# A pair's first four transposes, in the same step as its keys' sums (attention and a mixture of experts, one core)

## The chip, the cores and the metric

The kernel runs on one core of a Trainium2 chip. The time is device microseconds of one execution. The core's engines work side by side: TensorE (matmuls and transposes through the matrix array), ScalarE, VectorE, GpSimd, and SyncE, which here issues transfers. Each engine takes its instructions in the order in which the program emits them and waits by semaphores for the others.

## What is computed

Attention with random features for 4 batches of 8 heads (576 positions, 64 channels, 128 features), then four experts' two-layer networks on its output:

```python
def phi(x):
    proj = np.einsum('bhsd,md->bhsm', x, omega)
    sq = np.sum(x * x, axis=-1, keepdims=True) / 2.0
    h = proj - sq
    h = h - np.max(h, axis=-1, keepdims=True)
    return np.exp(h) / np.sqrt(m)
q_p, k_p = (phi(q_s), phi(k_s))
kv = np.einsum('bhsm,bhsd->bhmd', k_p, v)
z = np.sum(k_p, axis=2)
num = np.einsum('bhsm,bhmd->bhsd', q_p, kv)
den = np.einsum('bhsm,bhm->bhs', q_p, z)[..., None] + 1e-06
...
for e in range(E):
    h = np.maximum(x @ w1[e], 0.0)
    out += p[:, e:e + 1] * (h @ w2[e])
```

All is float32.

## The kernel before

Two heads make a pair, so each batch has four pairs. Batch 0 is done in an opening of its own (`begin`). The twelve pairs of batches 1 to 3 are cut into small steps by the generator `later_ticks`; each `yield` ends a step. The driver in `emit` runs the experts' work in pieces (a "visit" is one expert's half of its hidden units on a block of rows) and calls `next(ticks)` behind a piece as often as a fixed ratio says: 76 steps over 45.4 units of expert work for batches 1 and 2 (`over` is true), 54 steps over the first block of the larger visits for batch 3 (`over` is false). The order in which instructions are emitted is the order on each engine; nothing reorders it afterwards.

The steps of one pair, as far as they matter here:

- `project("q")` (L411): TensorE multiplies the queries with the features into two PSUM banks, one for each head. VectorE takes the maxima (L279, L284) and makes the bias (L289, L290).
- `exp_tails("q")`, `exp("q", 0)` (L417, L418): ScalarE makes the exponentials, two for the tails and four for the first head (L296). Then, a step later, `exp("q", 1)` (L424): four for the second head.
- `sum_keys()` (L430): TensorE accumulates the keys' sums (L310, L314; the trace has two records for each float32 matmul, 2 + 16), ScalarE copies them (L316), VectorE takes what the copy lost (L317). In the same step the next pair's values are loaded and its keys squared on GpSimd.
- `turn(0)` (L437): TensorE transposes four tiles of the queries' exponentials (L325): the first two of the first head, then the first two of the second head, into one PSUM bank. ScalarE copies it (L335) and VectorE takes the difference (L336). With `over`, the next pair's queries are squared on GpSimd in the same step.
- `turn(1)` (L441): the other four and the tail (L325, L329).

The results of `turn(0)` are used by `numerators(0)`, in the next pair's first step with `over`, and two steps behind `turn(0)` without.

The experts' matmuls are L674 to L676 and L867 (first layer), L689 to L691 and L942 (second layer); each weight tile is split into a high and a low part by ScalarE (L498) and GpSimd (L501). All PSUM tiles come from one pool of eight banks in turn.

Of the kernel before, what the change touches and what calls it, by code (L numbers as in the profile page):

```python
# [14 lines left out]
def attention_moe(ctx, tc, kT, qT, kd, qd, kn, qn, vn, omT, probs, w1, w2, out):  # L15
# [372 lines left out]
    def later_ticks(pairs, over):  # L388

        before = None  # L390
        for p, then in zip(pairs, pairs[1:] + [None]):
            p.project("k")
            p.project_tails("k")
            p.maxima("k")
            p.maxima_tails("k")
            p.bias("k")
            if before:
                before.numerators(0)
            yield
            p.exp_tails("k")  # L400
            p.exp("k", 0)
            p.lengths("q")
            if before:
                before.invert(0)
            yield
            p.exp("k", 1)
            if before:
                before.times(0)
                before.numerators(1)
            yield  # L410
            p.project("q")  # L411
            p.project_tails("q")
            p.maxima("q")
            p.maxima_tails("q")
            p.bias("q")
            yield
            p.exp_tails("q")  # L417
            p.exp("q", 0)  # L418
            if before:
                before.invert(1)  # L420
            if then:
                then.load("k")
            yield
            p.exp("q", 1)  # L424
            if before:
                before.times(1)
            if then:
                then.load("q")
            yield
            p.sum_keys()  # L430
            if then:
                then.load_v()
                if then.hp == 0:
                    then.load_tails()
                then.square("k")
            yield
            p.turn(0)  # L437
            if over and then:
                then.square("q")
            yield  # L440
            p.turn(1)  # L441
            if then:
                if over:
                    then.lengths("k")
                else:
                    then.square("q")
            yield
            if over and then:
                before = p
                continue  # L450
            before = None
            p.numerators(0)
            if then:
                then.lengths("k")
            yield
            p.invert(0)
            p.times(0)
            p.numerators(1)
            yield
            p.invert(1)  # L460
            p.times(1)
            yield
# [849 lines left out]
    def emit():  # L1312
        pairs, g1 = begin()
        later = [Halves(b, hp) for b in range(1, B) for hp in range(NP)]
        windows = {
            0: (first_rest(pairs, opening(later[0])), 15 / 11),
            3: (later_ticks(later[:-NP], True), 76 / 45.4),
            N0: (chain(opening(later[-NP]), later_ticks(later[-NP:], False)), 54 / (NV * (BIG[1][1] // P + 1) * 0.8)),
        }
        ticks, n, done, per = iter(()), 0, 0.0, 0  # L1320
        for v in range(len(visits)):
            if v in windows:
                for _ in ticks:
                    pass
                ticks, per = windows[v]
                n, done = 0, 0.0
            for share in first_visit(g1) if v == 0 else fast(v) if v >= N0 else plain(v):
                done += share
                while n < done * per:
                    next(ticks, None)  # L1330
                    n += 1
        store(0)
# [61 lines left out]
```

## Time and profile before

| | us |
|---|---|
| Median of 3 runs | 891.69 |
| Lowest and highest run | 889.99, 892.38 |
| The profiled execution | 892.62 |
| Its span, first to last instruction | 890.8 |
| TensorE busy | 884.1 |
| VectorE, GpSimd, ScalarE busy | 593.8, 566.3, 468.9 |

The span is 1.8 us shorter than the execution that it belongs to. Starts are in microseconds from the span's first instruction. A matmul's record is longer than the time that it holds TensorE, because matmuls overlap: how fast they go is read from one start to the next. A record that follows a wait or a block of short matmuls starts early, while its weights are loaded.

### The profile page before, as it was taken

Reading aid. Unit: us, or ns where it says so; the run is one execution under the profiler, and the core shown is the slowest. Engines: PE = TensorE matmul, PEld = TensorE weight load, DVE = VectorE, ACT = ScalarE, POOL = GpSimd, SP = SyncE. Lnnn points to the kernel's source line nnn. Section 1 sums busy time; section 2 is a strip of 40 time slices with the busy share of each in tenths; the row PEclk is TensorE's granted clock in tenths of the full one; section 3 lists DMA queues with packets and bytes.
Section 4 is the critical chain, followed back from the end, with each engine's and each line's share of the span. In section 5 each row is a group of like instructions: output and inputs, shape, how many; then the busy total and the mean of one; then the engine's idle time right before and its main releaser. Section 6 shows DMA issues by size and latency. Waiting matters only on the chain.

```text
span 890.8 us, 14823 instructions
## 1 busy us (share of the span) xinstructions
PE 884.1 (99%) x5484; PEld 789.4 (89%) x5484; DVE 593.8 (67%) x1026; ACT 468.9 (53%) x1038; POOL 566.3 (64%) x494
## 2 busy tenths in 40 slices
PE   9999999999999999999999999999999999999998
PEld 9988888888888898989889899898989898998988
DVE  5765566766767646586766666975848476675847
ACT  5564676776774564546545554634443435444442
POOL 6656465555634554444445346779898888979874
PEclk9999999999999999999999999999999999999999
DMA  6664454444521757436275353835152442425132
GB/s 179 165 204 153 127 170 135 150 154 137 160 80 60 254 154 274 181 135 246 77 273 175 111 211 111 305 117 165 48 178 87 139 157 80 155 60 178 44 135 95
DMA packets 64552, 134.01 MB, mean 150 GB/s; under 512 B 10624, under 2 KB 21056, under 8 KB 64480
## 3 DMA queue, kind: packets, MB, share of 16 engines
q1 hardware_dynamic: 54512, 102.95, 35.3%
q0 software_dynamic: 9360, 29.82, 10.3%
q8 instruction: 43, 0.70, 0.3%
q10 hardware_dynamic: 608, 0.30, 0.1%
q14 instruction: 29, 0.24, 0.1%
HBM read 98.96 MB, written 34.08 MB: 149 GB/s over the span
## 4 chain that ended last, share of the span: by engine, by line
PE 90%; DVE 4%; issue 2%; DMA 2%; ACT 1%; POOL 1%; SPq 0%; POOLq 0%; ACTq 0%; DVEq 0%
PE g L867 26%; PE g L942 17%; PE g L689 8%; PE g L691 7%; PE g L690 7%; PE g L674 3%; PE g L676 3%; PE g L675 3%; PE kv L314 2%; PE q_ps L266 1%; PE k_ps L266 1%; DMA kept<-w1ah 1%; PE qt_ps L325 1%; PE k_ps L147 1%; PE q_ps L147 1%
## 5 line engine op out<-in xcount | busy, mean ns | idle before, releaser
L501 POOL TENSOR_TENSOR w2l<-w2r,w2h 128x512 fp32r<-128x512 f32 x93 | 123.9, 1337 | 81.6 <-ACT w2h L498 69.8
L718 DVE SCALAR_TENSOR_TENSOR acc<-g,pr,acc 128x256 f32<-128x256 f32 (+1 forms) x278 | 139.2, 539 | 31.7 <-PE g L691 21.8
L501 POOL TENSOR_TENSOR w1sl<-w1r,w1sh 128x512 fp32r<-128x512 f32 (+1 forms) x43 | 75.2, 1749 | 72.3 <-ACT w1sh L498 56.8
L689 PE MATMUL g<-w2h,hh 128*128 128x512 f32 x280 | 112.7, 402 | 0.4 <-ACT kp L296 0.2
L691 PE MATMUL g<-w2h,hl 128*128 128x512 f32 x280 | 109.8, 392 | 0.0
L690 PE MATMUL g<-w2l,hh 128*128 128x512 f32 x280 | 109.5, 391 | 0.0
L879 DVE TENSOR_TENSOR sum<-g,sum 128x384 f32<-128x384 f32 (+1 forms) x96 | 59.3, 619 | 63.1 <-PE g L867 56.4
L892 DVE SCALAR_TENSOR_TENSOR hl<-sum,hh 128x384 fp32r<-128x384 f32 (+1 forms) x64 | 45.7, 717 | 81.7 <-ACT hh L888 52.3
L867 PE MATMUL g<-xbh,w1sh 128*128 128x384 f32 (+1 forms) x256 | 93.1, 364 | 0.0
L867 PE MATMUL g<-xbl,w1sh 128*128 128x384 f32 (+1 forms) x256 | 92.9, 363 | 0.0
L867 PE MATMUL g<-xbh,w1sl 128*128 128x384 f32 (+1 forms) x256 | 92.6, 362 | 0.0
L501 POOL TENSOR_TENSOR w1al<-w1r,w1ah 128x512 fp32r<-128x512 f32 (+1 forms) x45 | 51.5, 1159 | 52.1 <-ACT w1ah L498 36.7
L873 ACT ACTIVATE sum<-g 128x384 f32<-128x384 f32 (+1 forms) x96 | 50.7, 541 | 51.9 <-PE g L867 51.0
L867 PE MATMUL g<-xbh,w1ah 128*128 128x384 f32 (+1 forms) x192 | 70.1, 365 | 0.0
L498 ACT ACTIVATE w2h<-w2r 128x512 fp32r<-128x512 f32 x90 | 55.2, 627 | 28.2 <-DMA w2r<-in_w 22.1
L867 PE MATMUL g<-xbl,w1ah 128*128 128x384 f32 (+1 forms) x192 | 69.6, 362 | 0.0
L867 PE MATMUL g<-xbh,w1al 128*128 128x384 f32 (+1 forms) x192 | 69.5, 362 | 0.0
L691 PEld LDWEIGHTS g<-w2h,hl 128*128 128x128 f32 x280 | 52.5, 188 | 11.9 <-DVE hl L925 0.4
L689 PEld LDWEIGHTS g<-w2h,hh 128*128 128x128 f32 x280 | 52.7, 188 | 11.2 <-DVE sum L879 0.7
L690 PEld LDWEIGHTS g<-w2l,hh 128*128 128x128 f32 x280 | 52.7, 188 | 8.7
L888 ACT ACTIVATE hh<-sum 128x384 fp32r<-128x384 f32 (+1 forms) x64 | 35.0, 550 | 41.6 <-DVE sum L879 41.2
L867 PEld LDWEIGHTS g<-xbh,w1sh 128*128 128x128 f32 x256 | 48.1, 188 | 6.0 <-DVE sum L879 0.6
(212 smaller groups left out, 2438.5 us busy)
## 6 DMA issues: line engine op xcount, KB each, us to landing
w2r<-in_w SPq DMA_DIRECT2D x108, 256.0 KB, 2.9
w1r<-in_w SPq DMA_DIRECT2D x38, 512.0 KB, 3.6
kept<-w1sh SPq DMA_DIRECT2D x16, 512.0 KB, 4.9
kept<-w1sl SPq DMA_DIRECT2D x16, 512.0 KB, 5.5
w1sh<-kept POOLq DMA_DIRECT2D x16, 512.0 KB, 5.8
w1sl<-kept POOLq DMA_DIRECT2D x16, 512.0 KB, 6.6
kept<-w1ah SPq DMA_DIRECT2D x16, 384.0 KB, 4.3
kept<-w1al SPq DMA_DIRECT2D x16, 384.0 KB, 4.5
```

Of the source, the lines that this page charges most:

```text
L498: hi.activation(a, t, AF.Copy)
L501: lo.tensor_tensor(c, t, f32(a), ALU.subtract)
L689: nc.tensor.matmul(ps, ha[:, ts_], wa, start=(c == 0), stop=False)
L690: nc.tensor.matmul(ps, ha[:, ts_], wc, start=False, stop=False)
L691: nc.tensor.matmul(ps, hc[:, ts_], wa, start=False, stop=(c == FH - 1))
L718: nc.vector.scalar_tensor_tensor(to, ps, sc, to, ALU.mult, ALU.add)
L867: nc.tensor.matmul(ps, a[:, w], x[:, k], start=(start and k + at == 0), stop=(k == 1 and at == 2), skip_group_check=not start)
L873: nc.scalar.activation(t, P_[g][where], AF.Copy)
L879: nc.vector.tensor_tensor(t, P_[g][where], t, ALU.add)
L888: nc.scalar.activation(ha, t, AF.Relu)
L892: nc.vector.scalar_tensor_tensor(x, y, 0.0, f32(z), ALU.max, ALU.subtract)
L942: nc.tensor.matmul(to, x, w, start=(start and f + k == 0), stop=(f + k == 3), skip_group_check=not start)
```

## The change

The end of a step is moved behind `turn(0)`, so that the step of `sum_keys()` holds the four transposes and what follows them on ScalarE and VectorE too. The step behind it keeps the squaring of the next pair's queries where `over` is true (batches 1 and 2) and is empty in batch 3. The number of steps is as before.

```diff
                 if then.hp == 0:
                     then.load_tails()
                 then.square("k")
-            yield
             p.turn(0)
+            yield
             if over and then:
                 then.square("q")
             yield
```

## Rows read from the trace of the kernel before

**Rows 1.** The page: busy time of each engine, and the last chain by engine

```profile
PE 884.1 (99%) x5484; PEld 789.4 (89%) x5484; DVE 593.8 (67%) x1026; ACT 468.9 (53%) x1038; POOL 566.3 (64%) x494
...
PE 90%; DVE 4%; issue 2%; DMA 2%; ACT 1%; POOL 1%; SPq 0%; POOLq 0%; ACTq 0%; DVEq 0%
```

**Rows 2.** TensorE's waits: releaser, then us in total, times, longest us

```profile
PE g L942 <- DVE hl L925: 0.7, 2, 0.5
```

**Rows 3.** Timeline of TensorE, pair 1: start us, us, line, tiles, shape, count

```profile
99.83 0.39 PE L690 MATMUL g<-w2l,hh 128*128 128x512 f32 x1
100.05 0.39 PE L691 MATMUL g<-w2h,hl 128*128 128x512 f32 x1
100.28 0.60 PE L325 MATMUL qt_ps<-ident,qp 128*128 128x128 f32 x4
100.64 0.47 PE L689 MATMUL g<-w2h,hh 128*128 128x512 f32 x1
100.95 0.40 PE L690 MATMUL g<-w2l,hh 128*128 128x512 f32 x1
```

**Rows 4.** Timeline of TensorE in the opening, transposes right behind a pair's sums

```profile
19.51 0.61 PE L190 MATMUL qt_ps<-ident,qp 128*128 128x128 f32 x4
19.95 0.28 PE L147 MATMUL q_ps<-om,q 128*128 128x128 f32 x1
```

**Rows 5.** Timelines of ScalarE, weight loads and TensorE: TensorE waiting for exponentials

```profile
41.99 0.37 ACT L162 ACTIVATE qp<-q_ps,nm 128x128 f32<-128x128 f32 x1 [1.25 <-DVE nm L150]
...
42.41 1.17 PEld L190 LDWEIGHTS qt_ps<-ident,qp 128*128 128x128 f32 x5 [0.18 <-ACT qp L162]
...
385.70 0.50 PE L689 MATMUL g<-w2h,hh 128*128 128x512 f32 x1 [0.18 <-ACT kp L296]
386.04 0.39 PE L690 MATMUL g<-w2l,hh 128*128 128x512 f32 x1
```

**Rows 6.** Timelines of ScalarE and TensorE, pair 3

```profile
143.53 0.65 ACT L296 ACTIVATE qp<-q_ps,nbq 128x128 f32<-128x128 f32 x2
...
143.88 0.39 PE L675 MATMUL g<-x_first,w1sh 128*128 128x512 f32 x1
```

**Rows 7.** Timelines of VectorE, ScalarE and TensorE, pair 7

```profile
230.77 1.02 DVE L289 SCALAR_TENSOR_TENSOR mxq<-sqq,mxq 128x9 f32<-128x9 f32 x1
...
233.87 1.66 ACT L296 ACTIVATE qp<-q_ps,nbq 128x128 f32<-128x128 f32 x6
...
234.69 0.39 PE L675 MATMUL g<-x_first,w1sh 128*128 128x512 f32 x1
```

**Rows 8.** Timelines of GpSimd, VectorE, ScalarE and TensorE, pair 10

```profile
388.94 2.39 POOL L501 TENSOR_TENSOR w1sl<-w1r,w1sh 128x1024 fp32r<-128x1024 f32 x1 [5.33 <-ACT w1sh L498]
...
389.85 1.50 DVE L289 SCALAR_TENSOR_TENSOR mxq<-sqq,mxq 128x9 f32<-128x9 f32 x1
...
391.66 0.74 ACT L303 ACTIVATE qp<-t_ps,nbq 64x128 f32<-64x128 f32 x2 [2.79 <-DVE nbq L290]
...
393.73 0.39 PE L690 MATMUL g<-w2l,hh 128*128 128x512 f32 x1
...
395.11 0.61 ACT L296 ACTIVATE qp<-q_ps,nbq 128x128 f32<-128x128 f32 x2
```

**Rows 9.** Timelines of VectorE, ScalarE and TensorE, pair 12

```profile
497.43 1.88 DVE L289 SCALAR_TENSOR_TENSOR mxq<-sqq,mxq 128x9 f32<-128x9 f32 x1
...
500.36 1.66 ACT L296 ACTIVATE qp<-q_ps,nbq 128x128 f32<-128x128 f32 x6
...
501.05 0.39 PE L690 MATMUL g<-w2l,hh 128*128 128x512 f32 x1
```

**Rows 10.** Timelines of ScalarE and TensorE, pair 9

```profile
344.99 1.66 ACT L296 ACTIVATE qp<-q_ps,nbq 128x128 f32<-128x128 f32 x6
...
347.36 0.39 PE L690 MATMUL g<-w2l,hh 128*128 128x512 f32 x1
```

**Rows 11.** Bias line of the queries: duration ns min/median/max, first and last start

```profile
L289 DVE SCALAR_TENSOR_TENSOR mxq<-sqq,mxq x12: 169/170/1880, 94.1 to 497.4; 128x9 f32<-128x9 f32 x12
```

More of the change, by code (lines that the diff above doesn't have):

```diff
@@ L435, in later_ticks @@
                 then.square("k")
+            p.turn(0)
             yield
-            p.turn(0)
             if over and then:
```

## The prediction, made before the changed kernel was built or run

> **What bounds the kernel now.** I read the shares of the page first, then the list of TensorE's waits, then the order of TensorE around the edited lines. TensorE is busy for 884.1 of 890.8 us, and the chain that ended last is 90% TensorE [rows 1]. Nothing hides a TensorE stall: behind the opening the largest entry in the list of its waits is 0.7 us in two waits [rows 2]. So a microsecond in which TensorE stands still costs very nearly a microsecond, and the question is whether the new order makes it stand still.
>
> The reader should see next how TensorE runs there. In the first of the twelve pairs the sums of the keys are followed by six 512-column matmuls of the experts, then by the four transposes [rows 3], which show the last two of the six. The experts' matmuls start 0.22 to 0.24 us apart; I use 0.23. The change takes the matmuls that stand between sums and transposes and puts them behind the transposes; the rows show one pair, and in the trace all twelve have 6 to 24 such matmuls there, so the edit bites in every pair.
>
> **Part 1, TensorE's own work.** Nothing is added or removed. In the old place the four transposes cost, from 100.28 to the second matmul behind them at 100.95 less one step of 0.23, 100.72 - 100.28 = 0.44 us [rows 3]. In the new place they stand right behind fp32 matmuls of the sums. The opening has just that neighbourhood: sums end, transposes start at 19.51, the next matmul at 19.95, so 0.44 us again [rows 4]. Difference 0.00 per pair. The bounds come from the matmul behind a block of short ones, whose successor is 0.31 instead of 0.23 us away [rows 3]: if one such exit of 0.08 us went in each pair the gain would be 12 x 0.08 = 1.0 us, and if one were added it would be as large a loss. I take 0, since the transposes' 0.44 us already is that excess.
>
> **Part 2, the new wait.** The first two transposes read exponentials of the first head, the last two the first two of the four that ScalarE makes for the second head. Today the experts' matmuls stand between and cover that. In the new order they don't. I compare two times in each pair. F is when TensorE is through with the sums: the start of the second matmul behind them, less 0.23 (the first one's record begins early, while its weights load). E is when the second of the last four exponentials ends.
>
> Without a wait, F + 0.44 is where the next expert matmul streams. With one, TensorE goes on late: in the opening an exponential that starts at 41.99 and takes 0.37 is followed by the load of its transpose at 42.41, 0.05 after its end [rows 5]. Then the last transpose's load (0.11, the step in rows 4) is exposed, and so is the next matmul's: after a wait the first matmul is 0.34 from the second where 0.23 is normal, 0.11 more [rows 5]. So the next matmul streams at E + 0.05 + 0.22, and the loss is E - F - 0.17 where that is positive.
>
> - Pair 3: F = 143.88 - 0.23 = 143.65, E = 143.53 + 0.65 = 144.18. Loss 0.36 us [rows 6].
> - Pair 7: F = 234.69 - 0.23 = 234.46, E = 233.87 + 1.66 = 235.53. Loss 0.90 us [rows 7].
> - Pair 10: F = 393.73 - 0.23 = 393.50, E = 395.11 + 0.61 = 395.72. Loss 2.05 us [rows 8].
> - Pair 12: F = 501.05 - 0.23 = 500.82, E = 500.36 + 1.66 = 502.02. Loss 1.03 us [rows 9].
> - The other eight come out negative. The nearest is pair 9: E = 344.99 + 1.66 = 346.65 against F = 347.36 - 0.23 = 347.13, 0.65 us to spare [rows 10].
>
> Sum 4.3 us. What is queued behind the waiting transposes on TensorE is the whole expert stream, since it issues matmuls in order; later waits that could swallow part of it are the 0.7 us above, and those end on engines that TensorE itself feeds, so I let them absorb nothing.
>
> **Why E is late, and whether that will repeat.** In pair 10 VectorE's small bias instruction takes 1.50 us where the median of its line is 0.17 [rows 11]. It starts at 389.85 and ends at 391.35, and GpSimd's split of a weight tile runs from 388.94 to 391.33 [rows 8]. In pair 12 it is 1.88 us [rows 9], in pair 7 1.02 us [rows 7]. The exponentials wait for the bias: in pair 10 ScalarE stood idle for 2.79 us until it came [rows 8]. So the delays are inside E: 1.50 - 0.17 = 1.33 in pair 10, 1.71 in pair 12, 0.85 in pair 7.
>
> The Trainium skill, page "SBUF — State Buffer", section "SBUF: two separate sides", says that VectorE with two SBUF inputs and GpSimd contend for one pair of ports, which the first to start holds for its whole instruction while the other is blocked. The rows of pair 10 agree: the bias instruction ends 0.02 us after GpSimd's. By that rule the delay is the remainder of GpSimd's instruction and the sum is 4.3 us; if the two shared the ports, the delays would nearly go and the sum would be the 1.1 us of the rival below.
>
> The collisions sit before the edited step, between parts that the edit does not move: in pair 10 VectorE's additions feed ScalarE's split, that feeds GpSimd's, and the bias comes later in the same VectorE order. I therefore expect them to recur.
>
> **Part 3, the other queues.** ScalarE's copy of the transposes and VectorE's difference of it move ahead of the experts' next activations and accumulations, and the PSUM bank is taken one turn earlier. What stands behind is the ReLU of a hidden block (six steps of 0.23, so 1.4 us after the transposes, longer than the copy) or an accumulation, whose bank comes round eight turns later. So the cover is there; if it failed, the bound from the nearest rows is one bias-like collision of the same two engines, 1.3 us once, and below zero there is nothing to win, as TensorE waits for neither today [rows 2]. I take 0. No DMA moves; the loads, GpSimd's squares and SyncE's queue keep their places. In the last batch one step is left empty, which issues nothing.
>
> **Sum.** The profiled execution took 892.62 us, 1.8 more than its span of 890.8. 892.62 + 4.3 = 896.9. It is 0.93 us above the median of the runs (891.69), so for a median I say 896.0 us, 0.48% slower.
>
> **Rivals.**
> - *The collisions don't recur* (not slower). The place is the bias instruction in pairs 7, 10 and 12. Without them E is earlier by 0.85, 1.33 and 1.71: pair 7 loses 0.05, pair 12 nothing, pair 10 0.72, pair 3 still 0.36. Sum 1.1 us, median 892.8. It decides as soon as 1.6 us of the 4.3 goes, which takes two of the three collisions (0.85, 1.33 and 1.03 us of loss). Against it: the order that makes them is untouched; for it: they hang on starts that lie 0.9 us apart in pair 10 [rows 8]. Chance 0.13.
> - *The transposes wait for all of the last four exponentials.* Two more at a step of about 0.26 each, so 0.5 us in each of four pairs: 4.3 + 2.1 = 6.4, median 898.1. Pair 9 would still have 0.14 to spare. Against it, in the opening the first transpose's load starts 0.05 us after the first exponential, and the five loads follow at a step of (1.17 - 0.14) / 4 = 0.26, not all at once behind the last [rows 5]. Chance 0.11.
> - *The order matters to nothing*: the transposes' wait is covered because the last exponentials come earlier once ScalarE has one copy less in its way, or an exit is saved (part 1). 890.7 to 891.7. Against it: in pair 10 ScalarE had stood idle until the bias came [rows 8], so it is not a backlog of copies that makes E late. Chance 0.08.
>
> That the edit does nothing is excluded by the 6 to 24 matmuls counted above.
>
> **How the numbers follow.** Forecast 0.68, around 896.0 with about 1.3 either way (one pair's wait more or less). 0.3% is about what a measurement of this kernel can tell from no change: 2.7 us, so "slower" starts at 894.4. Slower: the forecast without its lower edge, 0.66, and the second rival, 0.11: 0.77. Same: 0.13 of the first rival, 0.05 of the third, 0.02 of the forecast's edge: 0.20. Faster: 0.03. The range goes from just below the first rival's 892.8 to just above the second's 898.1: 892.3 to 899.0.
>
> **What would show it.** In the changed kernel's TensorE waits a new line must stand, transposes waiting for the exponentials, with four entries (pairs 3, 7, 10 and 12), the longest near 2 us in pair 10, and eight pairs without any. The four transposes behind the sums should still take 0.44 us in those eight. The prediction is wrong if no such entry stands there, if the pairs that wait are others, or if the bias instruction has 0.17 us in pairs 7, 10 and 12.

## The result: slower by half a per cent

| | us |
|---|---|
| Changed kernel, median of 10 runs | 894.7 (892.94 to 896.27) |
| Kernel before, median of 10 runs on the same chip | 889.8 (888.57 to 892.57) |
| Ratio | 1.0052, 95% interval 1.0041 to 1.0063 |
| Profiled execution of the changed kernel, its span | 894.11, 892.3 |

The changed kernel is slower by 0.52%, 4.6 us of 889.8; the medians themselves lie 4.9 us apart. The spans of the two profiled executions differ by 1.5 us only, and that is not the change: the one of before had a slow opening (last section). So the comparison that follows runs from the first pair's sums to the last pair's last transpose. The view of one line's instructions has both ends; of the changed kernel (first two rows) and of the kernel before (last two; duration in ns, then first and last start in us):

```profile
L310 PE MATMUL kv<-vb,kp x24: 377/378/378, 94.7 to 500.1; 128*128 128x256 f32 x24
L329 PE MATMUL qt_ps<-ident,qp x12: 272/273/273, 100.5 to 509.5; 128*128 128x128 f32 x12
...
L310 PE MATMUL kv<-vb,kp x24: 377/378/378, 96.7 to 498.8; 128*128 128x256 f32 x24
L329 PE MATMUL qt_ps<-ident,qp x12: 272/273/273, 102.5 to 507.2; 128*128 128x128 f32 x12
```

That is 509.5 - 94.7 = 414.8 us, and in the kernel before 507.2 - 96.7 = 410.5 us. The stretch of the twelve pairs is 4.3 us longer.

The page and the list of TensorE's waits, after:

```profile
PE 883.4 (99%) x5484; PEld 788.1 (88%) x5484; DVE 593.6 (67%) x1026; ACT 467.6 (52%) x1038; POOL 564.5 (63%) x494
...
PE 83%; DVE 6%; ACT 4%; issue 3%; POOL 3%; DMA 1%; SPq 0%; POOLq 0%; ACTq 0%
...
PE qt_ps L325 <- ACT qp L296: 2.7, 4, 1.4
...
PE g L942 <- DVE hl L925: 0.7, 2, 0.5
```

TensorE does the same number of matmuls in the same busy time, to 0.7 us [rows 1]; the chain that ended last now passes through ScalarE, VectorE and GpSimd for 13% of the span where it was 6%. Behind the opening the list has one new line: transposes (L325) that wait for the exponentials (L296), four times. The entry of [rows 2] is unchanged.

Where they are is seen in TensorE's timeline: pair 1, which does not wait, and then pairs 3, 7, 10 and 12.

```profile
96.89 0.60 PE L325 MATMUL qt_ps<-ident,qp 128*128 128x128 f32 x4
97.24 0.48 PE L689 MATMUL g<-w2h,hh 128*128 128x512 f32 x1
97.56 0.40 PE L690 MATMUL g<-w2l,hh 128*128 128x512 f32 x1
...
141.68 0.38 PE L325 MATMUL qt_ps<-ident,qp 128*128 128x128 f32 x2
142.52 0.59 PE L325 MATMUL qt_ps<-ident,qp 128*128 128x128 f32 x2 [0.46 <-ACT qp L296]
...
143.18 0.40 PE L675 MATMUL g<-x_first,w1sh 128*128 128x512 f32 x1
...
233.32 0.39 PE L325 MATMUL qt_ps<-ident,qp 128*128 128x128 f32 x2
234.15 0.58 PE L325 MATMUL qt_ps<-ident,qp 128*128 128x128 f32 x2 [0.44 <-ACT qp L296]
...
234.81 0.40 PE L675 MATMUL g<-x_first,w1sh 128*128 128x512 f32 x1
...
393.18 0.38 PE L325 MATMUL qt_ps<-ident,qp 128*128 128x128 f32 x2
394.93 0.59 PE L325 MATMUL qt_ps<-ident,qp 128*128 128x128 f32 x2 [1.37 <-ACT qp L296]
...
395.59 0.39 PE L690 MATMUL g<-w2l,hh 128*128 128x512 f32 x1
...
502.14 0.55 PE L325 MATMUL qt_ps<-ident,qp 128*128 128x128 f32 x2
503.14 0.58 PE L325 MATMUL qt_ps<-ident,qp 128*128 128x128 f32 x2 [0.45 <-ACT qp L296]
...
503.79 0.39 PE L690 MATMUL g<-w2l,hh 128*128 128x512 f32 x1
```

In pair 1 the four transposes stand in one row and take 97.56 - 0.23 - 96.89 = 0.44 us, as in [rows 3] and [rows 4]. In the four others the row is split: two transposes of the first head, a gap, two of the second head. The gap that the profile prints in brackets is shorter than the loss, because a matmul's record goes on after the next one could have started (a transpose's record is 0.27 us, and in pair 1 the next one starts after 0.11). The loss is read as in the prediction, from the start of the second expert matmul less 0.23, less the first transpose's start, less 0.44: 143.18 - 0.23 - 141.68 - 0.44 = 0.83 in pair 3, and likewise 0.82 in pair 7, 1.74 in pair 10, 0.98 in pair 12. Together 4.4 us, which is the 4.3 of the whole stretch.

### The profile page after: what moved, and what is told of

Its sections match the earlier page's. It is cut to its first block, busy times and chain, and to the rows that moved or that the text cites. A ratio compares the mean times of both kernels' runs of the same rounds, so it can differ in the third digit from the quotient of the medians.

```text
span 892.3 us, 14822 instructions
## 1 busy us (share of the span) xinstructions
PE 883.4 (99%) x5484; PEld 788.1 (88%) x5484; DVE 593.6 (67%) x1026; ACT 467.6 (52%) x1038; POOL 564.5 (63%) x494
## 4 chain that ended last, share of the span: by engine, by line
PE 83%; DVE 6%; ACT 4%; issue 3%; POOL 3%; DMA 1%; SPq 0%; POOLq 0%; ACTq 0%
PE g L867 29%; PE g L942 17%; PE g L689 7%; PE g L691 7%; PE g L690 7%; PE g L674 2%; PE g L675 2%; PE g L676 2%; PE kv L314 1%; PE k_ps L266 1%; PE qt_ps L325 1%; PE kv L177 1%; PE q_ps L266 1%; PE nd L207 1%; POOL w2l L501 1%
```

## The experiments

The theory is that the cost is the wait of the transposes for the second head's exponentials, in four pairs. The rivals: that the order costs something in every pair (the copies of ScalarE and VectorE ahead of the experts' work, another neighbour for the transposes), and, behind the theory, that the exponentials are late for another reason than the collisions of VectorE and GpSimd. All ratios are to the kernel before, run beside them.

| Kernel | Ratio (95%) | Pairs' stretch, us | Transposes' waits in TensorE's list |
|---|---|---|---|
| before | 1 | 410.5 | none |
| the change | 1.0052 (1.0041 to 1.0063) | 414.8 | 2.7 us, 4 |
| pairs 3, 7, 10, 12 alone | 1.0060 (1.0044 to 1.0077) | 414.6 | 2.9 us, 4 |
| the other eight alone | 1.0001 (0.9989 to 1.0012) | 410.5 | none |
| transposes alone moved | 1.0056 (1.0040 to 1.0072) | 414.3 | 2.5 us, 4 |
| change, maxima in PSUM | 1.0011 (0.9998 to 1.0023) | 411.8 | 0.7 us, 2 |
| change, exponentials together | 1.0031 (1.0020 to 1.0042) | 412.4 | 0.9 us, 2 |
| change, both | 0.9997 (0.9988 to 1.0006) | 409.9 | none |
| before, both | 0.9990 (0.9979 to 1.0001) | 410.1 | none |

**In which pairs.** The change was cut in two, once for the pairs named and once for the rest:

```diff
-            p.turn(0)
+            early = (4 * p.b + p.hp - 3) in (3, 7, 10, 12)
+            if early:
+                p.turn(0)
             yield
+            if not early:
+                p.turn(0)
             if over and then:
                 then.square("q")
```

(`not in` for the other eight.)

> The change in pairs 3, 7, 10 and 12 alone; the other eight keep the order of before. If the cost is TensorE's wait for the last exponentials, all of it is here: those four waits stand in the trace of the changed kernel with 0.8, 0.8, 1.7 and 0.9 us, so 4.2 us and some 0.5% over the kernel before. If the new order costs something in every pair (copies of ScalarE and VectorE moved ahead, another neighbour for the transposes), a third of 4.6 us: 1.5 us, 0.2%.

> The change in the other eight pairs (1, 2, 4, 5, 6, 8, 9, 11) alone. If the cost is the wait, these have none and the time is that of before, within 1 us, with no wait of transposes for exponentials in TensorE's list. If each pair costs the same, two thirds of 4.6 us: 3.1 us, 0.35%.

The first costs what the change costs, 1.0060, and has the same wait (first row below); the second costs nothing, 1.0001, and the largest entry behind the opening in its list is the second row, the one of [rows 2]:

```profile
PE qt_ps L325 <- ACT qp L296: 2.9, 4, 1.6
```

```profile
PE g L946 <- DVE hl L929: 0.7, 3, 0.3
```

(The edit moves later lines by four.) Eight pairs with the new order, copies and all, are free; four carry the whole cost. An order that costs in every pair is out.

**The copies.** Here TensorE's transposes move as in the change, while the copies stay in the step where they were:

```diff
             p.turn(0)
             yield
+            p.turn_copies(0)
```

where `turn_copies` is the part of `turn` behind the transposes.

> TensorE's four transposes are moved as in the change, in all pairs; ScalarE's copy and VectorE's difference of them stay in the step where they were. If the wait is the cause, the time is that of the change, 4 to 5 us over before, with the same four waits in TensorE's list. If the copies that moved ahead on ScalarE and VectorE are the cause, the time is near that of before.

1.0056, and the wait stands (2.5 us, four times). The copies that moved ahead on ScalarE and VectorE have no visible part in it.

**Why the exponentials are late.** The maxima go into unused columns of the tails' PSUM bank, so that the two bias instructions (L289, L290) read only one operand from SBUF:

```diff
-            for x in ("mx", "nb"):
-                setattr(self, x + which, att.tile([P, 9], F32, tag=x + which, name=x + which))
+            setattr(self, "nb" + which, att.tile([P, 9], F32, tag="nb" + which, name="nb" + which))
+            setattr(self, "mx" + which, self.t_ps[0][:, 2 * M:2 * M + 9])
```

> The change, and the maxima of a projection in unused columns of its tails' PSUM bank in place of SBUF, so that the two bias instructions read one SBUF operand and one of PSUM. If they are late because they read two SBUF operands beside a split of GpSimd, the bias takes about 0.2 us in every pair, the waits in pairs 3, 7 and 12 go and pair 10 keeps 1.7 - 1.1 = 0.6 us: 0.6 us over before. If they are late for another reason, the four waits and the 4 to 5 us stay.

1.0011, with the four waits down to two. The bias line of this kernel, its VectorE and GpSimd in pair 10, its waits, and its TensorE in pairs 3 and 10:

```profile
L289 DVE SCALAR_TENSOR_TENSOR t_ps<-sqq,t_ps x12: 172/172/173, 93.4 to 498.0; 128x9 f32<-128x9 f32 x12
...
389.65 0.17 DVE L289 SCALAR_TENSOR_TENSOR t_ps<-sqq,t_ps 128x9 f32<-128x9 f32 x1
389.86 0.17 DVE L290 SCALAR_TENSOR_TENSOR nbq<-sqq,t_ps 128x9 f32<-128x9 f32 x1
...
388.10 2.41 POOL L501 TENSOR_TENSOR w1sl<-w1r,w1sh 128x1024 fp32r<-128x1024 f32 x1 [4.45 <-ACT w1sh L498]
...
PE qt_ps L325 <- ACT qp L296: 0.7, 2, 0.4
...
PE k_ps L266 <- DMA k<-in_kd: 0.6, 1, 0.6
...
142.65 0.38 PE L325 MATMUL qt_ps<-ident,qp 128*128 128x128 f32 x2
...
143.93 0.40 PE L675 MATMUL g<-x_first,w1sh 128*128 128x512 f32 x1
...
393.04 0.38 PE L325 MATMUL qt_ps<-ident,qp 128*128 128x128 f32 x2
...
394.51 0.39 PE L690 MATMUL g<-w2l,hh 128*128 128x512 f32 x1
```

GpSimd's split runs from 388.10 to 390.51. The bias instruction starts in the middle of it, as in [rows 8], and takes 0.17 us instead of 1.50: across all twelve pairs 172 or 173 ns, where [rows 11] had a maximum of 1880. The edit moves this instruction's output to PSUM too, but that is not the reason: the one behind it (L290) still writes to SBUF, runs beside the same split and takes 0.17 us as well. So two SBUF operands beside a GpSimd instruction were the cause of the long bias, and that part of the forecast, read there from rows, is now shown.

Pairs 7 and 12 don't wait any more. Pair 10 loses 394.51 - 0.23 - 393.04 - 0.44 = 0.80 us, where 0.6 was expected, and pair 3 143.93 - 0.23 - 142.65 - 0.44 = 0.61 us, where none was: the maxima in PSUM have a price, in the last section, which may be the reason. The wait for a transfer of keys (L266) is one that no other of these profiles has. With the two losses it comes to 2.0 us, while the stretch is only 1.3 us longer than before; the 0.4 us by which the stretch of "before, both" is shorter, with its maxima in PSUM too, is a part of the rest.

**ScalarE's order.** The last four exponentials are emitted right behind the first head's:

```diff
             p.exp("q", 0)
+            p.exp("q", 1)
             if before:
                 before.invert(1)
             ...
             yield
-            p.exp("q", 1)
             if before:
                 before.times(1)
```

> The change, and the last four exponentials of the queries one step earlier, right behind the four of the first head, so that no split of weights stands between them on ScalarE. If TensorE waits for the second of these four, pair 10 goes from 1.7 to about 0.1 us and pair 3 to none, while pairs 7 and 12, where they already follow each other, keep 0.8 and 0.9: 1.9 us over before in place of 4 to 5. If ScalarE's order is not what TensorE waits for, 4 to 5 us stay.

1.0031, and two waits are left, in pairs 7 and 12 (losses of 0.81 and 0.98 us). ScalarE in pair 10 of the change between the two heads' exponentials (first row), and ScalarE and TensorE of this kernel:

```profile
393.56 1.06 ACT L498 ACTIVATE w1sh<-w1r 128x1024 fp32r<-128x1024 f32 x1 [0.59 <-issue]
...
391.15 2.17 ACT L296 ACTIVATE qp<-q_ps,nbq 128x128 f32<-128x128 f32 x8
393.16 1.11 ACT L498 ACTIVATE w1sh<-w1r 128x1024 fp32r<-128x1024 f32 x1
...
392.52 0.67 PE L325 MATMUL qt_ps<-ident,qp 128*128 128x128 f32 x4
...
393.27 0.39 PE L690 MATMUL g<-w2l,hh 128*128 128x512 f32 x1
```

The split of a weight tile, 1.1 us of ScalarE behind 0.59 us in which it stood idle, was between the two heads' exponentials. Now it stands behind them, and the four transposes are one row: pair 10 loses 393.27 - 0.23 - 392.52 - 0.44 = 0.08 us, although its bias still takes 1.23 us. So in pair 10 the late bias and ScalarE's order carried the wait together: with the bias on time 0.80 us were left, with the other order almost nothing.

**Both, with the change and without it.**

> The change, with the maxima in PSUM and the last exponentials one step earlier. If both parts of the delay are understood, no transposes wait for exponentials and the time is that of before within 1 us; if the new order has a cost of its own, it is what is left.

> The kernel before with the same two edits (maxima in PSUM, last exponentials one step earlier) and without the change: what these edits cost or bring by themselves. Expected: nothing, within 1 us of before, since no transposes wait there. If exponentials that come earlier hold up a ReLU on ScalarE that TensorE waits for, it is slower by that, up to 1 us in a pair.

With both edits the changed order costs nothing: 0.9997, no transposes wait for exponentials, and its stretch is 409.9 us against 410.1 without the change. The cost of the change is its waits and nothing else that these runs can see (their intervals are about 1 us either way). The two edits by themselves bring at most 0.2%, and their interval reaches past 1: a faster kernel is not shown.

## Why the prediction was right

- **Part 1** (no change in TensorE's own work) holds: 0.44 us for the four transposes in the new place, and eight pairs that cost nothing.
- **Part 2** named the four pairs, and they are the four. Its sum was 4.3 us; measured are 4.4 in the rows of the waits, 4.3 over the stretch and 4.6 (3.6 to 5.6) by the ratio of the runs. Term by term it was less good: 0.36, 0.90, 2.05 and 1.03 forecast, 0.83, 0.82, 1.74 and 0.98 found. Two misses of about half a microsecond and of a third cancelled, and that is luck: the same four waits come to 4.6 us in the trace of "pairs 3, 7, 10, 12 alone" and to 4.1 in that of "transposes alone moved". The rule for the loss, E - F - 0.17, is good to 0.05 us: with E from the changed kernel's own trace (142.73, 234.36, 395.13 and 503.34) and F the start of the first transposes it gives 0.88, 0.87, 1.78 and 1.03. What was off is E.
- *Pair 3* was mis-sized because E was taken from one execution of the kernel before as fixed. In it a collision lies one stage earlier, at the bias of the keys, which the forecast had not looked at. GpSimd and VectorE there, before (two rows) and after (two rows):

```profile
128.60 2.54 POOL L501 TENSOR_TENSOR w2l<-w2r,w2h 128x512 fp32r<-128x512 f32 x2
130.60 0.56 DVE L289 SCALAR_TENSOR_TENSOR mxk<-sqk,mxk 128x9 f32<-128x9 f32 x1
```

```profile
127.16 2.54 POOL L501 TENSOR_TENSOR w2l<-w2r,w2h 128x512 fp32r<-128x512 f32 x2
128.61 1.12 DVE L289 SCALAR_TENSOR_TENSOR mxk<-sqk,mxk 128x9 f32<-128x9 f32 x1
```

  GpSimd's two splits end at 131.14 and 129.70, and the bias with them. VectorE came to it 2.00 us after GpSimd's start before and 1.45 after, so it waited 0.56 us longer. The exponentials of the keys, the ReLU behind them and the queries' bias follow later by the same half microsecond: the ReLU starts 141.44 - 137.23 = 4.21 us ahead of the pair's sums before, 139.47 - 135.78 = 3.69 after.

  The change is not needed for such a shift. Up to that bias the kernel with "pairs 3, 7, 10, 12 alone" emits in the order of before, and "the other eight alone" in the order of the change; the same instruction in their profiles:

```profile
130.69 1.08 DVE L289 SCALAR_TENSOR_TENSOR mxk<-sqk,mxk 128x9 f32<-128x9 f32 x1
```

```profile
130.32 0.34 DVE L289 SCALAR_TENSOR_TENSOR mxk<-sqk,mxk 128x9 f32<-128x9 f32 x1
```

  So one order gave 0.56 and 1.08 us, the other 1.12 and 0.34. With "transposes alone moved" it was 0.86, and pair 3 lost 0.57 us where it lost 0.83 in the change. The loss of pair 3 differs from one execution to the next by a quarter of a microsecond or more, and rows of one profile can't forecast it closer. What shifts GpSimd against VectorE stays open.
- *Pair 10* was over by 0.3: GpSimd's split began 1.19 us ahead of the bias instead of 0.91 [rows 8], so the collision was 1.23 us, not 1.50:

```profile
388.36 2.39 POOL L501 TENSOR_TENSOR w1sl<-w1r,w1sh 128x1024 fp32r<-128x1024 f32 x1 [5.06 <-ACT w1sh L498]
...
389.55 1.23 DVE L289 SCALAR_TENSOR_TENSOR mxq<-sqq,mxq 128x9 f32<-128x9 f32 x1
```

  Here the order of the other pairs seems to count. Where the eight pairs keep the old order the collision is 1.50 us (before, and "pairs 3, 7, 10, 12 alone", in which pair 10 lost 1.97 us, near the 2.05 forecast); where they have the new one it is 1.23 (the change, "the other eight alone", "transposes alone moved"). The forecast took it that the edit leaves the parts that collide where they were. That held for whether they collide, and by these five profiles not quite for how long; the way from the one to the other was not followed.
- **Why E is late** was right in its cause. Without the collisions the stretch is 411.8 us instead of 414.8, and pairs 3 and 10 still lose 0.61 + 0.80 = 1.4 of the 4.4 us; the first rival's price for that case was 1.1. Two terms of this price were off. Pair 3 was put at 0.36 without the collision of its keys' bias. Pair 7 was put at 0.05 and loses nothing, because the second bias instruction collides there too, which the forecast did not count; before:

```profile
231.82 1.21 DVE L290 SCALAR_TENSOR_TENSOR nbq<-sqq,mxq 128x9 f32<-128x9 f32 x1
```

  The traces agree with the rule that the prediction cites from the Trainium skill, page "SBUF — State Buffer", section "SBUF: two separate sides": with two SBUF operands the bias ends with GpSimd's instruction, and with one of them in PSUM it does not wait.
- **Part 3** (copies moved ahead are free) holds by the third experiment, to the width of its interval.
- **The sum** came out 1.3 us above the measured median. The base did that: 891.69 was the median of three runs, 889.8 is that of ten, 1.9 us lower. The difference of the medians, 4.9 us where 4.3 was forecast, took 0.6 of it back.

Of the rivals, the collisions came back in all three pairs. The one that waits for all four exponentials is out by the rows: in pair 10 the transposes go on at 394.93, when the first of the four, which starts at 394.52 and takes 0.35 us, has been over for 0.06 us and three of the four have not ended:

```profile
394.52 0.35 ACT L296 ACTIVATE qp<-q_ps,nbq 128x128 f32<-128x128 f32 x1
```

That the order matters to nothing is out by the four new waits and by the interval, 1.0041 to 1.0063.

## What to carry to other kernels

Here one engine is busy for 99% of the time and takes its work in order, and moving a step up cost only where the cover was needed. In such a case list, for each place, when the engine would arrive and when the last operand is ready, and sum the differences that are positive. Eight of the twelve pairs had 0.65 us to spare or more, and the other four made the whole cost. When an operand is late, follow it back to the first instruction that is longer than its median: here a 0.17 us instruction that took up to 1.9. And where a wait is the remainder of another engine's instruction, read it from more than one profile: with one and the same order it was 0.56 us in one execution and 1.08 in another.

## What the runs showed of the hardware beside that

- Moving one of two SBUF operands to PSUM frees VectorE of the collision, but it has a price. In pair 3 of that kernel the maxima take 0.72 us a step, one 0.03 behind the other's end, where into SBUF they overlapped at 0.60 (first three rows that kernel, last two before):

```profile
137.41 1.42 DVE L279 TENSOR_REDUCE t_ps<-q_ps 128x4 f32<-128x512 f32 x2
138.86 0.70 DVE L284 TENSOR_REDUCE t_ps<-t_ps 64x1 f32<-64x128 f32 x2
139.60 0.17 DVE L289 SCALAR_TENSOR_TENSOR t_ps<-sqq,t_ps 128x9 f32<-128x9 f32 x1
...
138.47 1.28 DVE L279 TENSOR_REDUCE mxq<-q_ps 128x4 f32<-128x512 f32 x2
140.30 0.17 DVE L289 SCALAR_TENSOR_TENSOR mxq<-sqq,mxq 128x9 f32<-128x9 f32 x1
```

  From the first maxima to the bias 139.60 - 137.41 = 2.19 us, against 140.30 - 138.47 = 1.83 before. That is 0.36 us more before E. Pair 3 lost 0.61 us there, 0.25 more than the 0.36 that the forecast had from the rows of before. In pair 10 the bias starts 390.82 - 389.65 = 1.17 us ahead of the pair's sums, against 390.97 - 389.55 = 1.42 in the change, so 0.25 later, and 0.2 more than expected was lost. The price fits both; it was not tried by itself.
- The opening of one and the same order takes 2.0 us more or less from one execution to the next: the first pair's sums start at 96.7 in the profile of before, at 94.7 in that of the change, and between 94.8 and 96.9 in the others. In the chain of the two profiles the opening hangs on different transfers, the features' in the first, a tile of keys in the second:

```profile
0.75 3.08 DMA om<-in_omT
```

```profile
3.82 3.77 DMA k<-in_kT
```

  Two single profiles of this kernel can't be compared by their spans where a few microseconds count. A stretch that begins behind the opening is steadier: 409.9 to 410.5 us in the four kernels in which no transposes wait.
